# State attention with a gated convolution: six identity products fewer ahead of the first state transpose

## Chip, cores and metric

The kernel runs on one core of one Trainium2 chip. The metric is the device time of one execution in microseconds (us), taken as the median of several runs. Smaller is better. One execution is also recorded by the hardware profiler; its records are the rows shown here.

## What is computed

There are eight batches and eight heads. Each head has 512 tokens and 32 state vectors of 64 values. The tokens attend to the state, the state attends to the tokens, and both results stand one behind the other, 544 rows of 512 channels per batch. These rows go through a gated layer: a causal convolution of five taps and a sigmoid give the gate, one weight matrix gives the values, and a second matrix projects their product.

```
scores  = x @ state.T / 8            a  = softmax(scores)     xread = a @ state
scores2 = state @ x.T / 8            a2 = softmax(scores2)    sread = a2 @ x
y    = concat(xread, sread) along the rows, heads side by side: (8, 544, 512)
gate = sigmoid(sum over k of conv_w[k] * (y delayed by 4 - k rows))
out  = (gate * (y @ w_val)) @ w_out
```

The layer's weights arrive as 64-bit floats; the kernel loads them as 64-bit words and makes 32-bit floats of them on the chip.

## The kernel before

The whole program is a list of small steps (a load, four transposes, one activation and so on) which the functions `batch`, `group`, `weights` and `tail` append to `steps`. The list `ORDER` (lines 31 to 66) then says by number in which order they are issued, and a letter behind a number names the engine of a step that has a choice (a for ACT, v for DVE, g for POOL). Each engine works through its own share of that order in sequence, so the order fixes what stands behind what on PE, ACT, DVE, POOL and SP. SP issues all loads and stores.

Of the steps, 33 are `warm_up` (line 240). Each one multiplies the 128 x 128 identity with itself twice into a tile named warm, which nothing reads:

```
def warm_up(i):
    for j in range(2):
        nc.tensor.matmul(get("warm", i)[:, j * P:(j + 1) * P], ident, ident, start=True, stop=True)
```

In the trace one such product is two matmul records with two weight loads, so a step is four records of line L243. Twenty-six of the 33 steps stand in one row on PE at the start: six that the order issues among the first loads, and twenty, steps 915 to 934, one behind the other. The other seven stand later: steps 935, 4 and 936 among the transposes of x that follow, 8 and 937 a little later, 9 in the middle of the program and 3 at its end.

The order around them is as follows. SP issues one load of x (two heads of batch 0), the convolution's weights, three quarters of w_val, the four loads of the state of batches 0 to 3 (`load_group`, line 268, tile sg), the last quarter of w_val, the other three loads of x for batch 0, a quarter of w_out and five more loads of x (four for batch 1, one for batch 2). It then waits, because the next quarter of w_out goes where a quarter of w_val stands until DVE has made floats of it (tile wv). PE's first work behind the identity products is step 48, `group_T` (line 274): four transposes of the state into the PSUM tile sgp. Behind it come the transposes of x for batch 0 (`x_T`, line 309, tile xTp), one group of four for each load, small products that spread the convolution's weights (`conv_spread`, line 257, tile cwbp), three of the identity steps, and the scores of batch 0 (`long_scores`, line 337, tile sc), which need the transposed x and the transposed state.

ACT copies sgp into the places that the scores read (`long_T`, tile sTl) and, between these copies, scales the quarters of w_val (`words_scale`, tile wc_v); DVE needs these scaled words for the next step of the conversion (`words_clamp` at L221, `words_join` at L226, `words_sign` at L231). A PSUM tile is one of eight banks, taken in turn; a tile may be written when the one eight places before it has been read.

Of the kernel before, what the change touches and what calls it, by code (L numbers as in the profile page):

```python
# [29 lines left out]
ENGINES = dict(a="ACT", v="DVE", g="POOL")  # L30
ORDER = """
0 50 1 107 10 18 53 11a 65 41 42a 12 5 13g 14 43 23 7 35 44v 15 24a 45 36a 25 37 46 2 6 47 26v 29 915 916 917 918 919
920 921 922 923 924 925 926 927 928 929 930 931 932 933 934 48 114 38v 106 19 104 64a 105 27 39 30a 55a 115a 20a 89
935 112 28 4 113a 52a 31 16 108 185 54a 188 21 110 32v 109a 111a 33 936 120 51a 17 186 116 40 90a 34 189 91 195 49a
22a 122 62 56 191 123 92g 133 187 60v 193 286 118 77 119 287 121 59 285 190a 117 131 58a 288 57a 130 124 139 192a 196a
194a 93 134a 63a 125g 61a 141a 197 198 78a 71 66v 201 132a 184 291 199 94 293 79 103 8 126 292a 135 83 294a 127 68 385
295 296a 202 289 290a 200 388 128g 67a 101a 203 937 297 205 136 142g 129 80v 301 214 145 303 386 204 140a 143 302 299
387 146a 215a 84a 298 206g 486 213 151 207 216 208 304 86v 144 81 209v 85 69 70a 152a 168 137 150 217a 148 72a 82 222
153 147 154 487 155a 87 218 225a 73 284 156 74g 149a 219 210 138a 300 484 169 316 97a 75 88 227 76 211a 317a 228 160
170a 157 230 158a 226 223a 212g 485 95a 224 229a 159v 98g 164 231 165 314 250a 249 171g 235 256 220 583 315a 232 221a  # L40
389 391 390a 395 251 237 233g 166a 392a 252 396a 161 167g 393 394a 318 253 234 313 421 319 422a 397 238 96g 236a 264
257 402 384 423 254g 162a 99a 268 403 398 399 255 260 163g 401 239 400 269 258a 270a 305 100g 424a 102g 242 240v 322
306g 325a 243a 307 413 323a 414a 259g 425 181 326 241 172 244 494 245 182a 320 173a 246 308 309g 324 404 321a 415 261
492 483 493a 247g 495a 488 175 262a 310 263g 327 586 176v 311a 342 312v 343a 178 248 416a 328 405g 335 344 368 265
271g 585 345 346 266a 179a 406 347g 489a 330 356 348 350a 490 337 364 331 174 332 365 267g 329a 349 360 407 338 333g
275 272 682 491a 351 334 276a 339 352 357 520 183 408g 353 409 685 336a 273a 358a 340g 354g 523a 359g 410a 341 274 426
521v 524 281 582 366a 412 177 361 427 428a 584 411g 278 367g 429 522 362a 355 430 434 436 282a 683 496 431 369 363g
437 417 780 497 459 432g 279a 370a 448 435a 498 418 499 500 371g 449a 503 450 455 280 438 451 504g 587 433 456 439g
452 441 378 591 505 440 457a 506 283 507g 453g 501 460 372 588a 373a 684 443 502 508 375 379v 592a 442a 277 525 454
461g 376a 444 445 512 467 526 528 529 589 458g 446g 513a 468 514 593 533 463 509a 515a 447 530 784 462g 781 511 180  # L50
535 527a 381 547 548a 536 590a 419 549 594a 595 537 382a 420a 550 377 464 619 469g 531g 551 510g 465g 532 599 782 534a
692 540 600 470g 596 622a 686 687a 566 601 693a 597 552g 688 620a 598 602 603g 562 553 621 613 690 623 541a 689a 567
554 691a 542 516 466g 604 694 783 517 543 605 699 700 606g 374 544 545g 696 614a 695 607 568a 480 555 481a 697 546
569g 471 482 472a 473 624 608a 791 785 698 538v 610 380 563 639 641 642 643 556a 557g 474 786a 625 9 558 518 539 475a
789 632 701 640a 633v 627 609g 519a 564a 611 634 628 612a 790a 644g 645 681 477 626a 661 635 559 646 636 653 702g 703
478a 560a 648 787 629 565g 712 637g 479 792a 788a 561g 662 649 718 713a 793 881a 719a 615 704 663a 650 797 795 630g
638 616 794 879a 647a 885a 664g 886v 631 573 710 705g 654 798 570 721a 720 651g 800 617 574a 801g 706 711a 722 796
571a 799 809 655a 707a 709 657 618a 723 731 732a 808 714 715 658 733 725a 724 652 579 659a 476 580a 581 726 734 708g
727 716 656g 665 660g 735 810a 811 736g 883a 717a 764 802 745 812a 728 729g 747 666 576 748 667a 730 577a 813 738 803
740 749 817 752 383 818a 668g 741 804g 814 756 746v 672 753 750g 737 742 805 754a 739a 751 757 760 673a 822 819 758a  # L60
674 755g 743g 820v 765 821 806a 575 759v 675 678 766a 744 844 572 846 830 832 815 807g 761 847 669 679a 833 831a 767g
816v 848 851 834 762a 855 837 880g 884g 845a 835v 763g 839 859 849g 882g 836 676a 677 840 823 841 825 838v 863 887a
826 888v 777 771 827 899 900 842g 856 843 901 904 857a 824a 772a 774 850 680 858v 828v 773 860 670a 671 902 864 865a
861g 862g 903 894 866g 829 768 889 852 905 778a 853a 890 769a 779 906 895 854g 891 873 892 907a 870 908v 893 578 896
874a 897a 898v 867 871a 872 875 770 912 775v 913a 914 868v 869 909 876 776 910a 911 877a 3 878
""".split()


# [666 lines left out]
```

## Time and profile before

| | |
|---|---|
| three runs, median (lowest to highest) | 241.32 us (241.07 to 242.23) |
| the profiled execution | 241.91 us |
| its span, first to last instruction | 240.1 us |
| busy share of the span: PE, DVE, ACT, POOL | 97%, 78%, 69%, 55% |
| the chain that ended last: PE, DVE, ACT, POOL | 86%, 5%, 4%, 3% |
| identity products (L243) | 132 matmul records, 18.8 us busy |

PE is the matrix engine and PEld its weight loads, DVE, ACT and POOL are the vector, scalar and general engines, and SP issues DMAs. A busy share counts the time in which an instruction of the engine was under way. The chain is followed back from the last instruction: at each step to what released it, or to the instruction before it on its engine; it tells which work set the end. An idle time in front of an instruction stands in brackets with what ended it. PEclk is the clock granted to TensorE, as a share of its upper level. Matmuls overlap in the pipeline, so the start-to-start distance, not the recorded length of one, is what a matmul costs.

### The profile page before, as it was taken

Reading aid. Unit: us, or ns where it says so; the run is one execution under the profiler, and the core shown is the slowest. Engines: PE = TensorE matmul, PEld = TensorE weight load, DVE = VectorE, ACT = ScalarE, POOL = GpSimd, SP = SyncE. Lnnn points to the kernel's source line nnn. Section 1 sums busy time; section 2 is a strip of 40 time slices with the busy share of each in tenths; the row PEclk is TensorE's granted clock in tenths of the full one; section 3 lists DMA queues with packets and bytes.
Section 4 is the critical chain, followed back from the end, with each engine's and each line's share of the span. In section 5 each row is a group of like instructions: output and inputs, shape, how many; then the busy total and the mean of one; then the engine's idle time right before and its main releaser. Section 6 shows DMA issues by size and latency. Waiting matters only on the chain.

```text
span 240.1 us, 5167 instructions
## 1 busy us (share of the span) xinstructions
PE 232.9 (97%) x2015; PEld 175.7 (73%) x2015; DVE 188.1 (78%) x296; ACT 165.0 (69%) x348; POOL 131.5 (55%) x103
## 2 busy tenths in 40 slices
PE   6999999989999999999999999999999999999994
PEld 6997675546568686668686668867777688889883
DVE  2645799969999899699699987979589779965610
ACT  2327988789888794975799678897985746443311
POOL 3000436145786957956888567976868676052000
PEclk9999999999999999999999999999999999999999
DMA  5993998060002400637150012110020302022235
GB/s 182 312 357 118 296 242 183 19 141 15 3 0 60 114 3 1 187 109 212 44 135 0 3 44 101 46 44 1 3 87 3 131 0 90 1 87 87 75 100 177
DMA packets 34550, 22.90 MB, mean 95 GB/s; under 512 B 26058, under 2 KB 29150, under 8 KB 34526
## 3 DMA queue, kind: packets, MB, share of 16 engines
q1 hardware_dynamic: 34526, 22.57, 30.9%
q8 instruction: 16, 0.26, 0.5%
q14 instruction: 8, 0.07, 0.1%
HBM read 13.65 MB, written 8.91 MB: 94 GB/s over the span
## 4 chain that ended last, share of the span: by engine, by line
PE 86%; DVE 5%; ACT 4%; POOL 3%; issue 2%; ACTq 0%; POOLq 0%; DVEq 0%
PE val L484 17%; PE op L492 13%; PE op L494 12%; PE op L493 12%; PE warm L243 7%; PE xTp L309 5%; PE srp L365 3%; PE xr L421 3%; PE sgv L287 3%; PE tval L544 2%; PE e2p L355 2%; PE sc L315 2%; PE sc L337 2%; ACT xT L162 2%; POOL sl L175 1%
## 5 line engine op out<-in xcount | busy, mean ns | idle before, releaser
L461 DVE SCALAR_TENSOR_TENSOR acc<-xr,cw,acc 128x511 f32<-128x511 f32 (+2 forms) x84 | 59.7, 740 | 11.4 <-ACT xt L457 6.6
L492 PE MATMUL op<-woh,gh 128*128 128x512 f32 x128 | 51.6, 403 | 0.5 <-DVE swl L295 0.5
L494 PE MATMUL op<-woh,gl 128*128 128x512 f32 x128 | 50.3, 393 | 0.0
L493 PE MATMUL op<-wol,gh 128*128 128x512 f32 x128 | 50.1, 391 | 0.0
L175 POOL TENSOR_TENSOR gl<-g,gh 128x512 fp32r<-128x512 f32 x29 | 38.6, 1331 | 13.4 <-ACT gh L162 13.0
L175 POOL TENSOR_TENSOR acc<-acc,last 128x508 f32<-128x508 f32 x24 | 31.7, 1323 | 11.0 <-DVE acc L461 2.9
L492 PEld LDWEIGHTS op<-woh,gh 128*128 128x128 f32 x128 | 24.0, 188 | 8.7 <-DVE swl L295 1.3
L162 ACT COPY o<-op 128x512 f32<-128x512 f32 x28 | 16.5, 590 | 20.2 <-PE op L494 14.8
L494 PEld LDWEIGHTS op<-woh,gl 128*128 128x128 f32 x128 | 24.0, 188 | 5.4
L493 PEld LDWEIGHTS op<-wol,gh 128*128 128x128 f32 x128 | 24.1, 188 | 4.7
L487 DVE SCALAR_TENSOR_TENSOR g<-sig,val 128x512 f32<-128x512 f32 x32 | 21.6, 675 | 2.9 <-ACT sig L473 2.4
L484 PE MATMUL val<-ah,swh 128*128 128x512 f32 x56 | 23.4, 418 | 0.0
L162 ACT CAST gh<-g 128x512 fp32r<-128x512 f32 x28 | 17.5, 629 | 7.6 <-DVE g L487 7.6
L484 PE MATMUL val<-ah,swl 128*128 128x512 f32 x56 | 22.1, 394 | 0.0
L484 PE MATMUL val<-al,swh 128*128 128x512 f32 x56 | 22.0, 394 | 0.0
L456 ACT ACTIVATE acc<-xr,cw 128x512 f32<-128x512 f32 x28 | 19.4, 701 | 2.5 <-PE xr L421 2.3
L243 PE MATMUL warm<-ident 128*128 128x128 f32 x132 | 18.8, 303 | 1.8 <-POOL ident masks.py:199 1.8
L175 POOL TENSOR_TENSOR sl<-sl,mx 128x1024 f32<-128x1024 f32 x8 | 16.3, 2034 | 7.6 <-DVE mx L394 7.6
L162 ACT COPY xT<-xTp 128x512 f32<-128x512 f32 x32 | 18.1, 599 | 3.0 <-PE xTp L309 2.9
L473 ACT ACTIVATE sig<-acc 128x512 f32<-128x512 f32 x28 | 18.0, 644 | 2.7 <-POOL acc L175 1.9
L175 POOL TENSOR_TENSOR ex<-ex,rc 128x1024 f32<-128x1024 f32 x7 | 13.4, 1917 | 11.7 <-DVE rc L406 8.0
L243 PEld LDWEIGHTS warm<-ident 128*128 128x128 f32 x132 | 18.0, 218 | 2.1 <-POOL ident masks.py:199 1.8
(124 smaller groups left out, 457.2 us busy)
## 6 DMA issues: line engine op xcount, KB each, us to landing
x<-x SPq DMA_DIRECT2D x32, 256.0 KB
out<-o SPq DMA_DIRECT2D x32, 256.0 KB
vw<-w_val SPq DMA_DIRECT2D x4, 512.0 KB
ow<-w_out SPq DMA_DIRECT2D x4, 512.0 KB
sg<-state SPq DMA_DIRECT2D x8, 64.0 KB
z<-state SPq DMA_DIRECT2D x16, 32.0 KB
out<-to SPq DMA_DIRECT2D x8, 64.0 KB
cww<-conv_w SPq DMA_DIRECT2D x1, 20.0 KB
```

Source lines behind the costliest of these rows:

```text
L162: nc.scalar.copy(out, in_)
L175: (nc.vector if e == "DVE" else nc.gpsimd).tensor_tensor(out, a, b, op=how)
L243: nc.tensor.matmul(get("warm", i)[:, j * P:(j + 1) * P], ident, ident, start=True, stop=True)
L309: nc.tensor.transpose(get("xTp", b, pr)[:, j * P:(j + 1) * P], t, ident)
L456: nc.scalar.mul(get("acc", b, pr), pt, cw[:, HALO, pr:pr + 1])
L461: nc.vector.scalar_tensor_tensor(acc[:, d:], get("xr", b, pr)[:, :S - d], cw[:, HALO - d, pr:pr + 1], acc[:, d:], op0=ALU.mult, op1=ALU.add)
L473: nc.scalar.activation(get("sig", b, pr), get("acc", b, pr), AF.Tanh, scale=0.5)
L484: nc.tensor.matmul(get("val", b, k), w, a, start=(i == 0), stop=(i == len(parts) - 1))
L487: nc.vector.scalar_tensor_tensor(get("g", b, k), get("sig", b, k), 1.0, get("val", b, k), op0=ALU.add, op1=ALU.mult)
L492: nc.tensor.matmul(pt, gh, woh[:, k], start=(k == 0), stop=False)
L493: nc.tensor.matmul(pt, gh, wol[:, k], start=False, stop=False)
L494: nc.tensor.matmul(pt, gl, woh[:, k], start=False, stop=(k == NPR - 1))
```

## The change

Steps 929 to 934, the last six of the twenty in the row, are left out of `ORDER`. Fourteen remain in the row, and 27 of the 33 in all. Every other step stands in the same order and on the same engine as before; the rest of the diff is the same text with other line breaks.

```
@@ -30,39 +30,39 @@
 ORDER = """
 0 50 1 107 10 18 53 11a 65 41 42a 12 5 13g 14 43 23 7 35 44v 15 24a 45 36a 25 37 46 2 6 47 26v 29 915 916 917 918 919
-920 921 922 923 924 925 926 927 928 929 930 931 932 933 934 48 114 38v 106 19 104 64a 105 27 39 30a 55a 115a 20a 89
-935 112 28 4 113a 52a 31 16 108 185 54a 188 21 110 32v 109a 111a 33 936 120 51a 17 186 116 40 90a 34 189 91 195 49a
+920 921 922 923 924 925 926 927 928 48 114 38v 106 19 104 64a 105 27 39 30a 55a 115a 20a 89 935 112 28 4 113a 52a 31
+16 108 185 54a 188 21 110 32v 109a 111a 33 936 120 51a 17 186 116 40 90a 34 189 91 195 49a 22a 122 62 56 191 123 92g
...
```

## Rows read from the trace of the kernel before

**Rows 1.** The page: the span; the last chain by engine.

```profile
span 240.1 us, 5167 instructions
PE 86%; DVE 5%; ACT 4%; POOL 3%; issue 2%; ACTq 0%; POOLq 0%; DVEq 0%
```

**Rows 2.** Chain in time: start us, us, what (second row: later window).

```profile
1.81 14.39 PE warm L243 x104
13.96 2.23 PE warm L243 x20
16.20 0.44 PE sgp L276 x4
...
18.80 0.44 PE xTp L309 x4
...
21.88 2.19 PE sc L337 x32
```

**Rows 3.** By stretch: us, PE, PEclk, DMA, GB/s; first L243 (PE, PEld).

```profile
1.80:3.80 2.00, 1.99 (x9) 2.00 (x10) 1.00 0.83 262
...
16.20:21.88 5.68, 5.68 (x44) 1.00 0.42 146
```

**Rows 4.** Loads: sizes; timeline (start, us); SP waits (total, times, longest).

```profile
x<-x SPq DMA_DIRECT2D x32, 256.0 KB
vw<-w_val SPq DMA_DIRECT2D x4, 512.0 KB
sg<-state SPq DMA_DIRECT2D x8, 64.0 KB
...
1.73 1.29 SPq L199 DMA_DIRECT2D vw<-w_val  x3
3.06 3.37 SPq L270 DMA_DIRECT2D sg<-state  x4
...
7.07 3.70 SPq L186 DMA_DIRECT2D x<-x  x3
...
21.32 0.34 SPq L199 DMA_DIRECT2D ow<-w_out  x1
...
SPq L199 <- DVE wv L231: 7.5, 2, 6.8
```

**Rows 5.** By stretch: us, PE, PEld, DVE, ACT, POOL, PEclk, DMA share, GB/s.

```profile
0.00:10.40 10.40, 8.59 (x54) 8.60 (x55) 3.37 (x8) 2.97 (x4) 2.17 (x13) 1.00 0.74 231
0.00:11.20 11.20, 9.39 (x61) 9.39 (x62) 4.16 (x10) 3.66 (x5) 2.17 (x13) 1.00 0.76 239
0.00:14.80 14.80, 12.99 (x93) 12.99 (x94) 7.21 (x16) 3.66 (x5) 2.17 (x13) 1.00 0.83 270
18.60:20.00 1.40, 1.40 (x13) 1.25 (x13) 0.34 (x3) 1.15 (x3) 0.00 (x0) 1.00 0.11 40
20.00:21.30 1.30, 1.30 (x11) 1.01 (x10) 1.30 (x4) 1.00 (x3) 0.00 (x0) 1.00 0.00 1
```

**Rows 6.** Timeline: start us, us, instruction, [idle before it <-what ended it].

```profile
10.41 0.43 DVE L216 TENSOR_SCALAR ws_v<-vw 128x512 int32<-128x512 int32 x1 [1.16 <-DMA vw<-w_val]
...
13.83 0.42 DVE L216 TENSOR_SCALAR ws_v<-vw 128x512 int32<-128x512 int32 x1
...
16.67 0.27 ACT L170 ACTIVATE sTl<-sgp 64x128 f32<-64x128 f32 x1 [5.52 <-PE sgp L276]
...
17.66 0.43 DVE L221 TENSOR_SCALAR wc_v<-wc_v 128x512 f32<-128x512 f32 x1 [3.41 <-ACT wc_v L170]
...
23.96 1.53 PE L309 MATMUL xTp<-ident,x 128*128 128x128 f32 x12
```

**Rows 7.** Waits, 16 to 120 us: total us, times, longest.

```profile
POOL al L175 <- DMA z<-state: 4.5, 1, 4.5
...
PEld val L484 <- issue: 2.4, 10, 0.2
```

**Rows 8.** DMA queues of the page: packets, MB, share of 16 engines.

```profile
q8 instruction: 16, 0.26, 0.5%
```

More of the change, by code (lines that the diff above doesn't have):

```diff
@@ L32 @@
 0 50 1 107 10 18 53 11a 65 41 42a 12 5 13g 14 43 23 7 35 44v 15 24a 45 36a 25 37 46 2 6 47 26v 29 915 916 917 918 919
-920 921 922 923 924 925 926 927 928 929 930 931 932 933 934 48 114 38v 106 19 104 64a 105 27 39 30a 55a 115a 20a 89
-935 112 28 4 113a 52a 31 16 108 185 54a 188 21 110 32v 109a 111a 33 936 120 51a 17 186 116 40 90a 34 189 91 195 49a
-22a 122 62 56 191 123 92g 133 187 60v 193 286 118 77 119 287 121 59 285 190a 117 131 58a 288 57a 130 124 139 192a 196a
-194a 93 134a 63a 125g 61a 141a 197 198 78a 71 66v 201 132a 184 291 199 94 293 79 103 8 126 292a 135 83 294a 127 68 385
@@ L37 @@
[L37 to L65, printed above, removed]
+920 921 922 923 924 925 926 927 928 48 114 38v 106 19 104 64a 105 27 39 30a 55a 115a 20a 89 935 112 28 4 113a 52a 31
@@ new lines @@
+16 108 185 54a 188 21 110 32v 109a 111a 33 936 120 51a 17 186 116 40 90a 34 189 91 195 49a 22a 122 62 56 191 123 92g
+133 187 60v 193 286 118 77 119 287 121 59 285 190a 117 131 58a 288 57a 130 124 139 192a 196a 194a 93 134a 63a 125g 61a
+141a 197 198 78a 71 66v 201 132a 184 291 199 94 293 79 103 8 126 292a 135 83 294a 127 68 385 295 296a 202 289 290a 200
+388 128g 67a 101a 203 937 297 205 136 142g 129 80v 301 214 145 303 386 204 140a 143 302 299 387 146a 215a 84a 298 206g
+486 213 151 207 216 208 304 86v 144 81 209v 85 69 70a 152a 168 137 150 217a 148 72a 82 222 153 147 154 487 155a 87 218
@@ new lines @@
+225a 73 284 156 74g 149a 219 210 138a 300 484 169 316 97a 75 88 227 76 211a 317a 228 160 170a 157 230 158a 226 223a
+212g 485 95a 224 229a 159v 98g 164 231 165 314 250a 249 171g 235 256 220 583 315a 232 221a 389 391 390a 395 251 237
+233g 166a 392a 252 396a 161 167g 393 394a 318 253 234 313 421 319 422a 397 238 96g 236a 264 257 402 384 423 254g 162a
+99a 268 403 398 399 255 260 163g 401 239 400 269 258a 270a 305 100g 424a 102g 242 240v 322 306g 325a 243a 307 413 323a
+414a 259g 425 181 326 241 172 244 494 245 182a 320 173a 246 308 309g 324 404 321a 415 261 492 483 493a 247g 495a 488
@@ new lines @@
+175 262a 310 263g 327 586 176v 311a 342 312v 343a 178 248 416a 328 405g 335 344 368 265 271g 585 345 346 266a 179a 406
+347g 489a 330 356 348 350a 490 337 364 331 174 332 365 267g 329a 349 360 407 338 333g 275 272 682 491a 351 334 276a
+339 352 357 520 183 408g 353 409 685 336a 273a 358a 340g 354g 523a 359g 410a 341 274 426 521v 524 281 582 366a 412 177
+361 427 428a 584 411g 278 367g 429 522 362a 355 430 434 436 282a 683 496 431 369 363g 437 417 780 497 459 432g 279a
+370a 448 435a 498 418 499 500 371g 449a 503 450 455 280 438 451 504g 587 433 456 439g 452 441 378 591 505 440 457a 506
@@ new lines @@
+283 507g 453g 501 460 372 588a 373a 684 443 502 508 375 379v 592a 442a 277 525 454 461g 376a 444 445 512 467 526 528
+529 589 458g 446g 513a 468 514 593 533 463 509a 515a 447 530 784 462g 781 511 180 535 527a 381 547 548a 536 590a 419
+549 594a 595 537 382a 420a 550 377 464 619 469g 531g 551 510g 465g 532 599 782 534a 692 540 600 470g 596 622a 686 687a
+566 601 693a 597 552g 688 620a 598 602 603g 562 553 621 613 690 623 541a 689a 567 554 691a 542 516 466g 604 694 783
+517 543 605 699 700 606g 374 544 545g 696 614a 695 607 568a 480 555 481a 697 546 569g 471 482 472a 473 624 608a 791
@@ new lines @@
+785 698 538v 610 380 563 639 641 642 643 556a 557g 474 786a 625 9 558 518 539 475a 789 632 701 640a 633v 627 609g 519a
+564a 611 634 628 612a 790a 644g 645 681 477 626a 661 635 559 646 636 653 702g 703 478a 560a 648 787 629 565g 712 637g
+479 792a 788a 561g 662 649 718 713a 793 881a 719a 615 704 663a 650 797 795 630g 638 616 794 879a 647a 885a 664g 886v
+631 573 710 705g 654 798 570 721a 720 651g 800 617 574a 801g 706 711a 722 796 571a 799 809 655a 707a 709 657 618a 723
+731 732a 808 714 715 658 733 725a 724 652 579 659a 476 580a 581 726 734 708g 727 716 656g 665 660g 735 810a 811 736g
@@ new lines @@
+883a 717a 764 802 745 812a 728 729g 747 666 576 748 667a 730 577a 813 738 803 740 749 817 752 383 818a 668g 741 804g
+814 756 746v 672 753 750g 737 742 805 754a 739a 751 757 760 673a 822 819 758a 674 755g 743g 820v 765 821 806a 575 759v
+675 678 766a 744 844 572 846 830 832 815 807g 761 847 669 679a 833 831a 767g 816v 848 851 834 762a 855 837 880g 884g
+845a 835v 763g 839 859 849g 882g 836 676a 677 840 823 841 825 838v 863 887a 826 888v 777 771 827 899 900 842g 856 843
+901 904 857a 824a 772a 774 850 680 858v 828v 773 860 670a 671 902 864 865a 861g 862g 903 894 866g 829 768 889 852 905
@@ L66 @@
+778a 853a 890 769a 779 906 895 854g 891 873 892 907a 870 908v 893 578 896 874a 897a 898v 867 871a 872 875 770 912 775v
+913a 914 868v 869 909 876 776 910a 911 877a 3 878
 """.split()
```

## Prediction

> **What bounds the kernel now.** I read the page's head and its chain first: 86% of the chain that ended last is PE work in a span of 240.1 us [rows 1]. The reader is to see there that time taken out of PE's own queue counts one for one, as long as what follows it is ready. So the question is local: are the removed products on the chain, how long are they, and is everything behind them ready that much earlier?
>
> The chain in order of time answers the first part. One unbroken piece of 104 identity matmuls runs from 1.81 to 16.20 us; right behind it, without a gap, come the state's first transposes (sgp), the first transposes of x, and so on to batch 0's scores, which start at 21.88 [rows 2]. The 104 records are 26 steps of four records each (two products, two records a product). These products wait for nothing but the identity, and nobody reads them. The removed six are the last of the 26.
>
> **What is taken away.** The price of a step has to be read where the six stand. The last 20 identity matmuls take 2.23 us, so 0.1115 us each and 0.446 us a step [rows 2]. The first 2 us of the same line hold only 9 of them, 0.22 us each, twice as much: that is TensorE's lower level of 1.2 GHz against 2.4 GHz later (the granted clock stands as 1.00 in that first stretch too, so the count of matmuls is what tells) [rows 3]. An average over all 26 steps (14.39 / 26 = 0.553 us) would thus price the six at 3.32 us, which is too much: they lie at the end, at the upper level. Six steps x 4 x 0.1115 = **2.68 us**. They issue no DMA and nothing on another queue. Each step takes one of the eight PSUM buffers in turn; the buffer of sgp was last held by an identity step eight places before it, and with 14 of the row left it still is, so no new wait for a buffer arises. That edit costs nothing.
>
> **What moves earlier, and whether it may.** sgp would start at 16.20 - 2.68 = 13.52 us. Four things have to be there in time.
>
> 1. The state itself (sg). Its four loads are issued from 3.06 us, behind one load of x and three of w_val [rows 4]. No view gives their landing, so I bound it by bytes (1 KB of the rows is 1,024 bytes). x and three w_val loads are 0.262 + 3 x 0.524 = 1.835 MB. DVE waited for the third of these w_val loads and started at 10.41 [rows 6]; by 10.40 the DMAs had moved 231 GB/s x 10.4 us = 2.402 MB [rows 5]. They are thus not served strictly in order: 0.567 MB of later loads were moved with them. Allowing sg the same excess, it is in when 1.835 + 0.262 + 0.567 = 2.664 MB are moved, which is at 11.2 us (239 x 11.2 = 2.677) [rows 5]. That is an estimate; the bounds are 9.5 us or so (strict order) and 16.2 us (PE did not wait for it there). I take 11.2, because the third w_val load is its neighbour in the queue. Margin: 2.3 us.
> 2. The other pieces of x for batch 0. Their three loads begin at 7.07 us [rows 4], behind the fourth w_val load. With the same excess they are in at 1.835 + 0.262 + 0.524 + 0.786 + 0.567 = 3.974 MB, about 14.8 us (270 x 14.8 = 3.996) [rows 5]. The second group of transposes of x stood at 18.80 [rows 2] and comes to 16.12. Margin: 1.3 us. The first group reads the load that was issued first of all. Batch 1's x transposes move from 23.96 [rows 6] to 21.28, and by 20.0 everything issued so far had landed: the DMAs stand still from 20.0 to 21.3 at 1 GB/s [rows 5].
> 3. ACT and DVE. ACT sits idle for 5.52 us before the copy of sgp at 16.67 and then does the next w_val scaling; DVE sits idle for 3.41 us until that scaling is done and goes on at 17.66 [rows 6]. Both are held by the identity products through sgp. With the change DVE could go on at 14.98; its last instruction before the idle time starts at 13.83 and is one of 0.42 us, so it ends at about 14.25 [rows 6]. Both engines move by the whole 2.68 us.
> 4. The DMA queue. SP stands for 6.8 us until DVE has finished a w_val piece, and issues the next w_out load at 21.32 [rows 4]; that becomes 18.64. What is left of the older transfers then is 40 GB/s x 1.4 us = 0.06 MB [rows 5], some 0.2 us at the 270 GB/s of the earlier stretch. So the loads that follow come 2.5 to 2.7 us earlier and stay ahead of their readers by nearly as much as now.
>
> Behind 24 us the work of all engines hangs on these same starts. The one wait on a DMA that stands high between 16 and 120 us is POOL's of 4.5 us for a load of z [rows 7], and that load is issued by SP, which moves with DVE. I therefore let the whole rest move: the gain is not given back unless one of the rivals holds.
>
> **An unknown.** PE has 48 instructions fewer (24 matmuls with 24 weight loads), so its instruction fetches, 16 packets on q8 over the span [rows 8], fall on other places of the program. No row shows a stall by a fetch. From both sides I allow 0.3 us, a little more than the usual 0.2 us of a gap marked "issue" [rows 7], and take zero.
>
> **The sum.** The profiled execution took 241.91 us, its span 240.1; 241.91 - 2.68 = 239.2. The median of the three runs is 241.32, 0.59 below the profiled one; from there 241.32 - 2.68 = 238.64. I forecast **238.6 us**, 1.1% faster. A difference under 0.5%, 1.2 us, cannot be told from none here.
>
> **Rivals.**
>
> *Data late (same).* If sg or the second piece of x lands later than my byte count has it, PE stands still where it now fills the time, and the gain shrinks to what is left: with sg at its upper bound of 16.2 us nothing is gained, 241.3; with x 1.5 us later than thought, 238.6 + 0.2. Against it speaks that ACT and DVE are the ones seen waiting, on PE, and that 2.677 MB had gone through the queue by 11.2 us [rows 5, 6].
>
> *Clock lost (slower).* Behind 16.20 PE's work is thinner: transposes, small matmuls, three steps of identity products left among them. If the granted clock fell there after the shorter row of dense products, all work up to the scores would run at 1.2 GHz: 21.88 - 16.20 = 5.68 us [rows 2] would take twice as long, as in the first 2 us [rows 3]. Against the gain of 2.68 that is +3.0 us: 244.3. It decides the sign from 2.7 us of PE-bound work at the lower level, and makes a measurable loss from 3.9 us. For it: the first stretch shows that the level depends on what PE did before. Against it: in the run before, the clock stays at 1.00 from 16.2 through 21.9 [rows 3], the rise lies long before the removed steps, and none of the removed steps stands inside the thin stretch; the products in it stay.
>
> The Trainium skill, "TensorE: Matmul & The Clock Gate", section "Part 4: PE-mode transpose", says that transposes do not count as PE activity for the clock in the way matmuls do. It speaks against taking dense products away ahead of a stretch of transposes, and by that rule the time would be this rival's. The trace agrees only so far that products were put among the transposes; with the thin stretch as it is, the clock held [rows 3], so I give the rule little weight.
>
> *Given back later (same).* PE's order is fixed, but ACT, DVE and POOL interleave the weights' preparation with batch 0 and 1. If a DMA, not these engines, set one of the later starts, a part of the 2.68 us would turn into a wait, at most the 2.68 (241.3). The busiest candidate is the stream of loads from 21.3 us on; it moves with SP, less 0.2 us, so I expect little.
>
> **How the numbers follow.** Forecast (whole shift): 0.85. Data late: 0.04. Given back in a larger part: 0.06. Clock lost: 0.05. In the forecast's case the three runs before spread from -0.25 to +0.91 us about their median, which gives 238.4 to 239.5; the fetches add 0.3 on either side, and a lost part of the shift lies above. The range is 238.0 to 239.9 us; a shift kept by half (240.0) or lost to the clock is left out, about 0.15 in all. Faster by over 0.5% (below 240.1): 0.87, the forecast with the half-kept shifts; within 0.5%: 0.08; slower: 0.05.
>
> **What would show it.** In the profile after: 80 identity matmuls in the first piece instead of 104; sgp at about 13.5 us with no idle time of PE before it; ACT's idle time before the sgp copy down from 5.5 to 2.8 us and DVE's from 3.4 to 0.7; SP's wait before the w_out load ended by DVE again, the load at about 18.6; batch 0's scores at about 19.2; a granted clock of 1.00 throughout; and a span of about 237.4. I would be wrong if PE waits on a DMA before sgp or before the transposes of x, if the clock falls between 13 and 25 us, or if scores start at 19.2 and the span is still above 238.5: then a later wait has taken it back.

## The result, and the profile after

| | before | after |
|---|---|---|
| median of three runs | 241.32 us (241.07 to 242.23) | 238.41 us (238.18 to 239.06) |
| the profiled execution | 241.91 us | 239.06 us |
| its span | 240.1 us | 237.3 us |

The ratio is 0.988, with a 95% interval from 0.9849 to 0.991: between 2.2 and 3.6 us less. The forecast was 238.6 us in a range of 238.0 to 239.9.

The page of the changed kernel gives the span, the instructions (48 fewer) and the chain by engine:

```profile
span 237.3 us, 5119 instructions
PE 86%; ACT 4%; DVE 4%; POOL 3%; issue 1%; ACTq 0%; POOLq 0%; DVEq 0%
```

The chain in order of time of the changed kernel (start us, us, what) answers to [rows 2]:

```profile
1.81 11.66 PE warm L243 x80
13.48 0.44 PE sgp L276 x4
...
16.08 0.44 PE xTp L309 x4
...
19.16 2.19 PE sc L337 x32
```

The row has 80 records instead of 104 and is 14.39 - 11.66 = 2.73 us shorter; sgp starts at 13.48 instead of 16.20, the second group of x transposes at 16.08 instead of 18.80, the scores at 19.16 instead of 21.88. Each has moved by 2.72 us, and nothing stands between the row and sgp. The stretch from sgp to the scores takes 5.68 us in both.

Busy time in that stretch of the changed kernel (us, PE, PEld, DVE, ACT, POOL, PEclk, DMA share, GB/s) answers to [rows 3]: the granted clock is 1.00, the upper level of 2.4 GHz.

```profile
13.48:19.16 5.68, 5.68 (x44) 4.83 (x43) 2.93 (x7) 4.41 (x10) 0.00 (x0) 1.00 0.76 266
```

The timeline of the changed kernel (start us, us, instruction, idle time before it and what ended it) answers to [rows 6], with SP's load of w_out from [rows 4]:

```profile
13.16 0.42 DVE L216 TENSOR_SCALAR ws_v<-vw 128x512 int32<-128x512 int32 x1
...
13.95 0.27 ACT L170 ACTIVATE sTl<-sgp 64x128 f32<-64x128 f32 x1 [3.46 <-PE sgp L276]
...
14.95 0.43 DVE L221 TENSOR_SCALAR wc_v<-wc_v 128x512 f32<-128x512 f32 x1 [1.37 <-ACT wc_v L170]
...
18.61 0.34 SPq L199 DMA_DIRECT2D ow<-w_out  x1
...
21.25 1.53 PE L309 MATMUL xTp<-ident,x 128*128 128x128 f32 x12
```

ACT, DVE and SP have moved with PE: 16.67 to 13.95, 17.66 to 14.95, 21.32 to 18.61, and batch 1's transposes from 23.96 to 21.25. The idle time of ACT and DVE before them has shrunk but has not closed, so neither is the limit yet.

The span is 2.8 us shorter in the profile, 0.1 us more than the shift at sgp. The rest goes with an instruction behind 40 us, where DVE and POOL meet; the last section comes to it.

### The profile page after: what moved, and what is told of

Same layout as the page of the kernel before. It is cut to its first block, busy times and chain, and to the rows that moved or that the text cites. A ratio compares the mean times of both kernels' runs of the same rounds, so it can differ in the third digit from the quotient of the medians.

```text
span 237.3 us, 5119 instructions
## 1 busy us (share of the span) xinstructions
PE 230.1 (97%) x1991; PEld 172.9 (73%) x1991; DVE 187.8 (79%) x296; ACT 165.0 (70%) x348; POOL 131.8 (56%) x103
## 4 chain that ended last, share of the span: by engine, by line
PE 86%; ACT 4%; DVE 4%; POOL 3%; issue 1%; ACTq 0%; POOLq 0%; DVEq 0%
PE val L484 17%; PE op L492 13%; PE op L494 12%; PE op L493 12%; PE warm L243 6%; PE xTp L309 5%; PE srp L365 3%; PE xr L421 3%; PE sgv L287 3%; PE tval L544 2%; PE e2p L355 2%; PE sc L315 2%; PE sc L337 2%; ACT xT L162 2%; POOL sl L175 1%
## 5 line engine op out<-in xcount | busy, mean ns | idle before, releaser
L162 ACT COPY o<-op 128x512 f32<-128x512 f32 x28 | 16.5, 590 | 20.2 <-PE op L494 14.8
L175 POOL TENSOR_TENSOR al<-sl,ah 128x1024 fp32r<-128x1024 f32 x6 | 14.4, 2402 | 7.4 <-DMA z<-state 4.2
L309 PE MATMUL xTp<-ident,x 128*128 128x128 f32 x128 | 18.1, 276 | 0.0
```

The costliest lines, as they stand in the source:

```text
L162: nc.scalar.copy(out, in_)
L175: (nc.vector if e == "DVE" else nc.gpsimd).tensor_tensor(out, a, b, op=how)
L309: nc.tensor.transpose(get("xTp", b, pr)[:, j * P:(j + 1) * P], t, ident)
```

## Experiments

Each kernel is the one before with another `ORDER`; times of one group were taken on the same chip beside runs of the kernel before. "Row" is the run of identity steps ahead of sgp that begins with step 915: twenty before, fourteen after.

| run | row | other edit | median, us (lowest to highest) | before, us | ratio, 95% interval |
|---|---|---|---|---|---|
| e4_row26 | 26 | | 243.55 (243.48 to 244.61) | 241.37 | 1.0096 (1.0073 to 1.0118) |
| e8_row14 | 14 | (the changed kernel) | 239.24 (238.22 to 239.59) | 241.93 | 0.9895 (0.987 to 0.992) |
| e5_row11 | 11 | | 237.22 (237.07 to 237.83) | 241.93 | 0.9821 (0.9797 to 0.9844) |
| e1_row8 | 8 | | 237.48 (236.16 to 238.01) | 241.37 | 0.9837 (0.9802 to 0.9873) |
| e6_row8_again | 8 | | 237.24 (236.81 to 237.79) | 241.93 | 0.9812 (0.9789 to 0.9835) |
| e2_row0 | 0 | | 241.61 (239.96 to 243.34) | 241.37 | 1.001 (0.998 to 1.0041) |
| e3_row14_no3 | 14 | three later steps out | 238.03 (237.52 to 238.5) | 241.37 | 0.9868 (0.9843 to 0.9892) |
| e9_row11_no3 | 11 | three later steps out | 237.37 (236.66 to 237.58) | 241.59 | 0.9815 (0.9793 to 0.9837) |
| e7_row5_state_first | 5 | state loaded first | 236.86 (236.49 to 239.95) | 241.93 | 0.9832 (0.9786 to 0.9877) |
| e10_row8_state_first | 8 | state loaded first | 236.51 (236.4 to 237.41) | 241.59 | 0.9798 (0.9772 to 0.9824) |

**The same price in the other direction, and again.** Six steps more:

```
-931 932 933 934 48
+931 932 933 934 938 939 940 941 942 943 48
```

> The kernel before with six steps more in the row (26 instead of 20). Theory: each step costs its 0.446 us on the chain, in this direction too: 2.68 us longer than before, 244.0 us, everything behind the row shifted as a whole. Rival, a part of the row is hidden by something that ends at the same time: less than 1 us longer.

And the changed kernel once more, on another chip:

```
-925 926 927 928 929 930 931 932 933 934 48
+925 926 927 928 48
```

> The changed kernel itself (fourteen steps in the row), on the same chip as the three runs beside it, for comparison. Theory: 2.68 us less than the kernel before, about 238.6 us; the first state transposes at 13.5 us.

The chains of the two runs, first the one with 26 steps, then the one with fourteen (start us, us, what):

```profile
1.81 17.12 PE warm L243 x128
18.93 0.44 PE sgp L276 x4
```

```profile
1.81 12.02 PE warm L243 x80
13.82 0.44 PE sgp L276 x4
```

With 26 steps sgp stands at 18.93, 2.73 us later than before, and the median is 243.55 - 241.37 = 2.18 us longer (1.8 to 2.9 by the interval, 2.68 expected). With fourteen the median is 241.93 - 239.24 = 2.69 us shorter. So a step of the row is on the chain in both directions, at about its price. What stands behind the row moves as a whole: from the start of the first transposes of x, right behind sgp, to the end of the span it is 223.3 to 223.6 us in all eight profiles in which the clock held and the three later steps were left in, though those transposes start anywhere from 10.99 us (first run with eight steps) to 19.36 us (26 steps).

The second fence also shows how far one execution can be from another: the same 80 records take 12.02 us here and took 11.66 us in the first profile, all of it in the part of the row that runs at the lower level, because the level rose later (between 6.8 and 7.8 us there are 7 records of the row instead of 10). A third of a microsecond is therefore nothing to be explained, and the profiles below differ by more.

**How far the row can shrink.** Three steps fewer than after, then six fewer (twice):

```
-923 924 925 926 927 928 929 930 931 932 933 934 48
+923 924 925 48
```

> Nine of the twenty steps in the row are left out (eleven stay). Theory: the state is still in before PE arrives, at 16.20 - 9 x 0.446 = 12.19 us, so all nine count: 4.0 us less than before, 1.34 less than with fourteen, about 237.2 us, with no wait of PE before the state transposes. Rival, the later loads of x take the gain back: less than 0.5 us under the run with fourteen, with PE waiting on a load of x.

```
-923 924 925 926 927 928 929 930 931 932 933 934 48
+48
```

> Twelve of the twenty steps in the row are left out (eight stay), with nothing else changed. Theory (the row is on the chain and the state's load sets how far it can shrink): twelve steps would be 12 x 0.446 = 5.36 us, but the state is in only at about 11.2 us by the byte count, so the first state transposes start at 11.0 to 11.3 with a short wait of PE on the loads of the state, and the gain against the kernel before is 4.9 to 5.2 us: about 236.3 us. Rival, data of x late: the second group of x transposes would come at 13.8 against an estimated landing of 14.8, PE waits there about 1 us, 237.4 us. Rival, clock lost: the thin stretch runs at the lower level, 5.7 us longer, about 242 us.

> The kernel with eight steps in the row again, whose timed runs lay 1.1 to 1.9 us above its profiled one. Theory: with eight steps PE arrives when the state lands, and both times differ from run to run (the rise of the clock to its upper level at 5.2 us in that profile against 7.0 to 7.2 us in the others, each us later delaying the row's end by half a us): spread of over 1 us, median 237.0 to 237.6, at most 0.5 us under the run with eleven; in the profile a wait of PE on the state's loads of 0 to 0.6 us and a granted clock of 1.00 behind it. Rival, the clock is lost in some executions: mean granted clock below 0.99 in some of the runs.

The timelines of PE around sgp, in the run with eleven steps, in the first with eight and in the second with eight:

```profile
11.46 0.60 PE L276 MATMUL sgp<-ident,sg 128*128 128x128 f32 x4
```

```profile
10.36 0.63 PE L276 MATMUL sgp<-ident,sg 128*128 128x128 f32 x4 [0.43 <-DMA sg<-state]
```

```profile
11.85 0.63 PE L276 MATMUL sgp<-ident,sg 128*128 128x128 f32 x4 [2.08 <-DMA sg<-state]
```

With eleven steps PE does not wait, as expected, and the kernel is 237.22 us, 2.0 us under fourteen steps where 1.34 were expected (the two intervals leave room for either). In the profiles sgp lies 13.82 - 11.62 = 2.20 us earlier than with fourteen on the same chip, as the chain of the run with eleven shows:

```profile
1.81 9.81 PE warm L243 x68
11.62 0.44 PE sgp L276 x4
```

Twelve records at the upper level account for 1.34 of it; the other 0.86 us is that the level rose earlier in this execution than in that one (11 records of the row between 5.8 and 6.8 us instead of 7), and is no gain of the edit. With eight, PE waits for the state, 0.43 us in one profile and 2.08 in the other: the end of the gain is the landing of the state, as the theory says, but that landing moves by 1.5 us between two executions of one kernel, on two chips (10.36 and 11.85). The expectation of the first run, 236.3 us, came true in the profiled execution alone (236.16); the timed runs were at 237.3 to 238.0. The second run's median of 237.24 is that of eleven steps. So three steps fewer than eleven gain nothing that can be measured, and the mean granted clock of every run with eight steps was 0.997 or more: the rival that the clock is lost does not explain the missing microsecond.

The second expectation put the spread on two things, the landing and the moment at which the level rises, and the wait at 0.6 us at most; 2.08 was measured. The length of the row does vary, 8.1 and 8.0 us for the same 56 records in these two profiles and 8.9 in that of the last run below, but even 8.9 would end it at 10.7, and the latest rise of all profiles (12.02 us for 80 records, so 12.02 - 24 x 0.1115 = 9.34 for 56) at 11.2. By the 223.5 us that always follow, the three timed runs of the first group (spans of 235.5 to 236.2 us) had sgp at about 11.4 to 12.1, an estimate: later than either end of the row, and near the landing of the second profile. So the late landing is the likelier cause of the missing microsecond; no trace of those timed runs shows it.

**Without the row.** All twenty out; six steps at the start stay:

```
-915 916 917 918 919 920 921 922 923 924 925 926 927 928 929 930 931 932 933 934 48
+48
```

> All twenty steps of the row are left out; the six identity steps among the first loads stay, and PE then stands idle until the state is in. Theory: the state transposes start at the same 11.0 to 11.3 us as with eight steps in the row, so data alone would give 236.3 us; but PE stands idle for some 4 us before them, the granted clock is then at its lower level in the stretch up to the scores, which takes about 5.7 us longer: about 242 us. Rival, the clock does not hang on these products: 236.3 us, within 0.5 us of the run with eight steps.

PE's timeline of this run, its chain, and busy time by stretch (us, PE, PEld, DVE, ACT, POOL, PEclk, DMA share, GB/s); lines of its code are numbered one lower:

```profile
10.91 1.11 PE L275 MATMUL sgp<-ident,sg 128*128 128x128 f32 x4 [3.70 <-DMA sg<-state]
```

```profile
10.91 1.11 PE sgp L275 x4
12.02 0.85 PE xTp L308 x4
...
21.62 3.13 PE sc L336 x32
```

```profile
7.00:10.40 3.40, 0.21 (x2) 0.00 (x1) 2.19 (x6) 1.24 (x2) 0.00 (x0) 1.00 1.08 277
10.40:13.00 2.60, 2.09 (x9) 1.76 (x10) 2.60 (x6) 1.02 (x3) 0.00 (x0) 0.50 1.07 383
13.00:19.80 6.80, 6.80 (x28) 5.75 (x29) 3.35 (x8) 3.18 (x8) 0.00 (x0) 0.50 0.73 263
19.80:24.00 4.20, 4.20 (x32) 2.72 (x36) 0.44 (x1) 1.95 (x5) 0.00 (x0) 0.50 0.81 272
24.00:30.00 6.00, 5.91 (x72) 3.70 (x66) 4.50 (x9) 4.79 (x13) 2.25 (x4) 0.99 0.84 266
```

Here the rival of the prediction is seen at work. sgp starts at 10.91, 2.6 us earlier than after the change, but PE has stood for 3.70 us, the granted clock has gone to 0.50 (1.2 GHz) at 10.4 and stays there until about 24. The four sgp transposes take 1.11 us instead of 0.44, and from sgp to the scores it is 21.62 - 10.91 = 10.71 us instead of 5.68: 5.03 us more, near the 5.68 that doubling gives. The median is that of the kernel before. PE is busy without a gap from 10.9 us on, with transposes, small matmuls and three identity steps, and that work, at which the upper level held when PE came to it without a wait, did not bring the level back: it rose at about 24 us, some 2.4 us after the scores had begun. From sgp to the end of the span it is 240.7 - 10.91 = 229.8 us instead of 237.3 - 13.48 = 223.8. The mean granted clock was 0.972 to 0.979 in all ten runs.

**The three steps inside the thin stretch.** With fourteen in the row and steps 935, 4 and 936 left out, and the same with eleven:

```
-925 926 927 928 929 930 931 932 933 934 48 114 38v
+925 926 927 928 48 114 38v
...
-935 112 28 4 113a
+112 28 113a
...
-936 120
+120
```

> The changed kernel, and the three identity steps among the transposes of x and in front of batch 0's scores left out as well. Theory: they cost 3 x 0.446 = 1.34 us of PE time, but the copies of the transposed x on ACT set the scores' start, and ACT is idle there for only some 0.65 us; gain 0.3 to 0.7 us against the changed kernel: about 237.9 us, the clock staying at its upper level. Rival, clock lost in the thin stretch without them: some 3 to 5.7 us longer, 241 to 244 us, with the granted clock below 1.00 between 14 and 25 us.

> Eleven steps in the row, and the three identity steps among the transposes of x and ahead of batch 0's scores left out. Theory (the row and the three steps act on different waits, so the gains add): 237.2 us with eleven, less 0.5 for the three (0.8 in the profile of the run with fourteen): 236.5 to 236.9 us where the kernel before takes 241.9, the clock held. Rival, the clock is lost now that both rows are shorter: some runs at 239 us or more with a mean granted clock below 0.99.

The chain of the run with fourteen, then that of the run with eleven:

```profile
13.56 0.45 PE sgp L276 x4
...
18.10 2.45 PE sc L337 x32
```

```profile
2.58 8.55 DMA vw<-w_val
...
11.15 0.43 DVE ws_v L216
...
12.85 0.61 DVE ws_v L226
...
13.48 0.68 ACT wc_v L170
...
16.62 0.59 ACT xT L162
...
17.26 2.45 PE sc L337 x32
```

With fourteen, the scores begin 18.10 - 13.56 = 4.54 us behind sgp instead of 5.68, but PE waits 0.24 us for ACT before them; what follows is 0.8 us earlier than after the change in the profile (batch 0's first maximum on DVE at 20.95 instead of 21.75). The medians tell less: 0.9868 here and 0.9895 for the changed kernel overlap. The clock held (mean granted clock 0.999 in the profiled execution). With eleven the gains do not add: 0.9815 against 0.9821 without this edit, and 237.37 us where 236.5 to 236.9 were expected. The chain of that run says why: it no longer goes through PE's row at all, but through the landing of a w_val load, DVE's and ACT's conversion of it, and the copies of x behind that on ACT. DVE works from 11.15 us on without a pause, so the idle time that it still had after the change is used up; ACT still has some (0.76 us before the copy of sgp). But this execution also had a late load and a long row: ACT takes up that w_val piece at 11.21 us where it did at 10.15 in the run with eleven steps alone, and the 68 records take 10.33 us instead of 9.81. How much of the missing gain is owed to that stays open. The clock was 1.00 in all five runs, so it was not the loss.

The Trainium skill, "TensorE: Matmul & The Clock Gate", section "Part 4: PE-mode transpose", which says that transposes do not count as activity for the clock as matmuls do, had been put beside the rival. These two runs do not show it as a danger here: without a single identity product among the transposes the clock stays up. The run without the row fits it: the same stretch, with PE busy from 10.9 us on, did not raise the clock, although three identity steps were in it.

**Another order of the loads.** The four loads of the state ahead of w_val, with five steps in the row and with eight:

```
-0 50 1 107 10 18 53 11a
+0 50 1 107 10 47 18 53 11a
...
-46 2 6 47 26v 29 915
+46 2 6 26v 29 915
...
-920 921 922 923 924 925 926 927 928 929 930 931 932 933 934 48
+48
```

(that is the one with five; the one with eight keeps 920, 921 and 922)

> Five steps stay in the row, and the four loads of the state are issued ahead of the loads of w_val instead of behind three of them. Theory (the state's landing is what ends the gain): the state is in before 7 us, PE does not wait for it, the state transposes start at 9.3 to 10 us and the second group of x transposes at 12 to 12.6, about when its load lands: 235.8 to 236.4 us, 1.2 us or more under the run with eight steps. Rival, the loads of x are next: PE waits about 1 us for the second piece, 236.9. Rival, eleven dense steps are too few for the clock: 240 us or more, the granted clock at its lower level in part of the stretch up to 25 us.

> Eight steps in the row and the state's loads issued ahead of w_val. Theory: without the wait for the state all twelve steps count, 5.36 us less than before, 236.5 us where the kernel before takes 241.9; the state transposes at 10.4 to 11.4 us, no wait of PE on the state, none or under 0.3 us on x, the clock held because PE does not stand still. Rival, the loads of x have become the limit, as with five steps: 237.0 or more with a wait of PE on x. Rival, the clock is lost in some executions as with five steps: runs up to 240 us.

PE's timeline with five steps, and its busy time by stretch (columns as above):

```profile
8.89 0.60 PE L276 MATMUL sgp<-ident,sg 128*128 128x128 f32 x4
...
12.79 0.89 PE L309 MATMUL xTp<-ident,x 128*128 128x128 f32 x4 [1.13 <-DMA x<-x]
```

```profile
10.40:13.00 2.60, 1.47 (x12) 1.18 (x11) 2.27 (x6) 0.95 (x2) 0.00 (x0) 1.00 1.06 372
13.00:19.80 6.80, 6.80 (x39) 5.07 (x41) 4.22 (x10) 5.59 (x13) 0.00 (x0) 0.50 0.98 313
19.80:24.00 4.20, 4.20 (x56) 3.35 (x56) 3.22 (x8) 2.51 (x8) 1.17 (x3) 1.00 0.98 363
```

The chain with eight steps:

```profile
1.81 8.90 PE warm L243 x56
10.71 0.44 PE sgp L276 x4
...
13.31 0.44 PE xTp L309 x4
...
16.39 2.23 PE sc L337 x32
```

With five steps the state is no longer late, sgp starts at 8.89, and the next load is: PE waits 1.13 us for the second piece of x. In this execution and one other of the six the clock was lost (mean granted clock 0.986 and 0.977, times 238.91 and 239.95 us); the other four took 236.5 to 237.1. Both rivals of the expectation thus came about, the wait for x and, in two of the six, the loss of the clock; the median of 236.86 is that of the first rival (236.9). The fall comes at 13 us, behind the wait, and the level is back at about 19.8, again after the scores have begun (18.42). With eight steps PE finds the state and x in place, the scores start at 16.39, 2.77 us earlier than after the change, the clock holds, and the median is 236.51 us, 241.59 - 236.51 = 5.08 less than before where 5.36 were expected. That is the fastest kernel of the case, though its interval overlaps those of eight and eleven steps without the new order, so the order of the loads is not shown to gain anything.

## Why the prediction was right

**The price.** The six were priced at the rate of the row's end, 0.446 us a step, 2.68 in all. The profile has the row 2.73 us shorter. The average of the whole row would have given 3.32. On the other chip the median fell by 2.69. That the first median lies 0.2 us beside the forecast is in part luck: the three runs of either kernel spread over 0.9 us or more, and six steps in the other direction moved the median by 2.18.

**That everything behind may move.** sgp, the transposes of x, ACT, DVE and SP moved by 2.71 to 2.72 us each, and the 223.3 to 223.6 us behind them held in every profile with the clock kept and the later steps in. The estimate of the state's landing is borne out by the runs that reached it: it was put at 11.2 us, and PE was seen waiting until 10.36, 10.91 and 11.85. The margin of 2.3 us was thus nearer 1.6 (13.48 - 11.85). The last pieces of x were put at 14.8 us. Only the first of those three loads was ever waited for, until 12.79 us in the run with five steps; no run reached the estimate for the last.

**ACT and DVE.** Their idle time was forecast to shrink to 2.8 and 0.7 us and shrank to 3.46 and 1.37: the w_val work ahead of it ran about 0.67 us earlier in this execution (DVE's last instruction starts at 13.16 instead of 13.83), with the loads. Their cover held with room; DVE's was used up only with eleven steps and the three others out.

**The unknown of the instruction fetches.** Taken as zero; no wait shows them after either.

**The rivals.** *Data late* is real but begins at about eight steps, six fewer than the change leaves. *Clock lost* is real too: it costs about what was reckoned for it, 5.0 against 5.7 us. But it was seen only in runs in which PE stood in wait for a load (3.70 us without the row, 1.13 us with five steps), and in the changed kernel PE does not stand between 1.81 and 19.16 us. Those runs are also the ones with the shortest rows, so whether the standing, the short row or both bring the fall is not shown. Where the prediction said that a shorter row of dense products ahead of the thin stretch might bring the loss, that alone did not: with eleven steps, also without identity steps in the stretch, the clock held in all runs (mean granted clock 0.997 or more). *Given back later* did not happen: the shift at the end is that at sgp, and 0.1 us more.

## What to carry to other kernels

Work that fills a wait is free only as long as the wait lasts: estimate the landing from the bytes ahead in the queue, and trim the filling to the latest landing, not to the mean. Price a removed piece at the rate of the place where it stands, not at the average of its group. And keep a little of the filling: here the last three steps between eleven and eight bought nothing, while without the filling PE stood for 3.7 us, and the lower clock behind that cost 5 us up to the scores, as much as all that could be gained. Moving the awaited load ahead in the queue gave the shortest median, but not clear of the noise, and with a row of five steps the next load was awaited instead.

## What the runs showed of the hardware

The 0.1 us beyond the shift goes with one instruction of DVE. Timelines of the kernel before, of the changed kernel, and of the changed kernel on the other chip:

```profile
46.10 0.61 POOL L221 TENSOR_SCALAR wc_o<-wc_o 128x512 f32<-128x512 f32 x1 [6.36 <-ACT wc_o L170]
46.15 0.83 DVE L216 TENSOR_SCALAR ws_o<-ow 128x512 int32<-128x512 int32 x1
```

```profile
43.39 0.95 POOL L221 TENSOR_SCALAR wc_o<-wc_o 128x512 f32<-128x512 f32 x1 [6.37 <-ACT wc_o L170]
43.43 0.43 DVE L216 TENSOR_SCALAR ws_o<-ow 128x512 int32<-128x512 int32 x1
```

```profile
43.73 0.61 POOL L221 TENSOR_SCALAR wc_o<-wc_o 128x512 f32<-128x512 f32 x1 [6.36 <-ACT wc_o L170]
...
43.77 0.86 DVE L216 TENSOR_SCALAR ws_o<-ow 128x512 int32<-128x512 int32 x1
```

The two start within 0.05 us of each other, and one of them takes its time alone while the other takes about 0.4 us more. Which one loses differs between two executions of the same kernel (second and third fence), so it is no effect of the change. The Trainium skill, "SBUF — State Buffer", section "SBUF: two separate sides", says that DVE, in some kinds of its instructions, and GpSimd share a pair of ports as an exclusive lock, and that the one that starts later is blocked for the whole instruction of the other. The trace agrees in that one of the two is held up, by 0.83 - 0.43 = 0.40 us (DVE) or 0.95 - 0.61 = 0.34 us (POOL). It does not show the rule of the first start: POOL has the earlier start in all three fences and loses in the second, though a difference of 0.04 us between two recorded starts may be too little to tell who was first. When DVE is held up, the starts behind it are 0.4 us later for some ten microseconds. At the end 0.1 to 0.2 us are left of it: of the eight profiles named above, the three in which POOL is held up have 223.3 to 223.4 us behind the row, the five in which DVE is have 223.4 to 223.6.

The other thing not expected is the one-sidedness of the clock: the stretch of transposes and small matmuls keeps the upper level when it begins at it and PE does not wait for a load in it (1.00 from 13.48 to 19.16 after the change) and stays at the lower when it begins there (0.50 until about 24 us without the row, PE busy from 10.9 on). What brings the fall stays open. It fell in the profile with a wait of 1.13 us (five steps, the wait in the middle of the thin stretch) and not in the one with 2.08 us (eight steps, the wait ahead of it), so the length of the wait alone does not decide it.

The rise of the level at the start is not fixed either. The same 56 records of the row took 8.0, 8.1 and 8.9 us in three executions, 68 records 9.81 and 10.33, and 80 records 11.66 and 12.02. Comparisons of single executions with one another carry up to about 0.9 us from this alone, a third of what the change is worth.
